# Attention and a SoLU layer on one core: the stationary operands of the two projections get fixed places in SBUF

## The chip, the cores and the metric

The kernel runs on one core of one Trainium2 chip. The metric is the device time of one execution in microseconds (us). Five engines work side by side: TensorE (PE; its weight loads are listed apart as PEld), VectorE (DVE), ScalarE (ACT), GpSimd (POOL) and SyncE (SP, which here only issues transfers). SBUF is the on-chip memory that they read from; a tile has the same byte address in each of its 128 partitions, and "place" below is that address. PSUM is where matmuls write.

## What is computed

The input is q, k, v for a batch of 4, 8 heads, 768 positions and 64 values a head. Each position attends to its neighbours within a window of 16 and to 24 block summaries of the keys (maxima) and values (means). The result is put in rows of 512 values, 3,072 of them, and goes through a layer of two projections:

```python
h = x @ w_in                                   # 3072x512 by 512x1024
e = np.exp(h - h_max)
sm = e / (np.sum(e, axis=-1, keepdims=True) + 1e-09)
solu = h * sm
ln = (solu - mu) / np.sqrt(var + 1e-06) * g_ln
return (ln @ w_out).astype(np.float32)         # 3072x1024 by 1024x512
```

## The kernel before

The 3,072 rows are cut into 24 tiles of 128 rows (t = 0 to 23). For each tile the attention of a quarter of the heads and positions is prepared some tiles ahead: scores (`s`, line 578), a transposition of the exponentials (`t`, line 633), and the values (`x`, line 672). Then `first(t)` (line 686) computes h = x times w_in, the SoLU and the normalization; `turn(t)` (line 750) transposes the normalized rows; and `second(t)` (line 765), four tiles behind, computes the output o.

Both projections work on numbers that are split in an upper part and a lower part, each in a 32-bit format that TensorE takes in one pass. The upper part of x is `xh`, its lower part `xl`; of the normalized rows they are `lh` and `ll`; a weight piece `w` holds both parts, 2,048 bytes each. Three matmuls of 512 columns make one product (lines 697 and 775):

```python
for n, (a, i) in enumerate(((hi, 1), (lo, 0), (hi, 0))):
    nc.tensor.matmul(hp.ap, a.ap[:, c, ts], w.ap[:, i], ...)
```

The first operand (x or the rows) is the stationary one: it is loaded into the array in slices of 128 columns, 512 bytes in a partition. The weight piece is the moving one and streams through. Each tile has 8 such triples in h and 8 in o, so 24 matmuls each.

The order of all work is found ahead of time, in Python. `Plan.op` records each operation with its estimated cost and what it reads and writes; `Plan.order` simulates the engines and orders the operations by due time, in 64 tries with noise; `Plan.issue` (line 141) then emits them in the order of the best try and puts filling matmuls (line 900) where TensorE would idle early on. Costs and due times don't depend on where a tile lies.

`Plan.buf` (line 93) gives each tag a ring of slots. The tile of a slot is made only when it is first used, at `Buf.ap`, and a pool lays its slots one behind the other in that order, each rounded up to 32 bytes. The pool `const` comes first, with a few constants and the 16 weight slots of 4,096 bytes; the pool `sb` lies right behind it. This gives these places, as the remainder of the address by 512:

| tile | slots | remainder by 512 before | used by |
|---|---|---|---|
| w (both parts) | 16 | 96 | h and o, moving |
| xh | 2 | 160, 32 | h; slot by t//2 even, odd |
| xl | 2 | 160, 32 | h; slot by t//2 even, odd |
| lh | 2 | 160, 352 | o; slot by t even, odd |
| ll | 2 | 352, 96 | o; slot by t even, odd |

`lh` and `ll` also take the first value rows that are loaded (`load_v_rows`, line 443), six loads in all, so that the rows of tile t land in slot t mod 2 in both rings. `vacc` (line 496) is a tile of 256 bytes with sums of values.

Of the kernel before, what the change touches and what calls it, by code (L numbers as in the profile page):

```python
# [13 lines left out]
BF16 = mybir.dt.bfloat16  # L14
# [37 lines left out]
class Buf:  # L52


    def __init__(self, make, prev=()):
        self.make, self.prev, self.tile = make, prev, None
        self.ops, self.writers, self.readers, self.gone = [], {}, {}, False
# [15 lines left out]
class Plan:  # L73
# [14 lines left out]
    TRIES, NOISE = 64, 3.0  # L88

    def __init__(self):  # L90
        self.ops, self.rings, self.banks, self.idle = [], {}, {}, None

    def buf(self, pool, shape, dtype, tag, bufs, name):
        ring = self.rings.setdefault(tag, [])
        slot = f"{tag}_{len(ring) % bufs}"
        b = Buf(lambda: pool.tile(shape, dtype, tag=slot, bufs=1, name=name), ring[-bufs:][:1] if len(ring) >= bufs else ())
        ring.append(b)
        return b

    def place(self, make, bank, tag):  # L100

        b = Buf(make, [self.banks[bank]] if bank in self.banks else ())
        self.banks[bank] = b
        self.rings.setdefault(tag, []).append(b)
        return b
# [149 lines left out]
def attn_then_solu(ctx: ExitStack, tc: tile.TileContext, q, k, v, vr, vb, w_in, w_out, g_ln, out):  # L255
# [4 lines left out]
    plan = Plan()  # L260
# [161 lines left out]
    kraw, ksum, vsum, vst, vacc = {}, {}, {}, {}, {}  # L422
    qt, vt, xh, xl, es, ats = {}, {}, {}, {}, {}, {}
# [414 lines left out]
    for t in range(NT):  # L838
        n, j = divmod(t, 2)
        b, g = its[n]  # L840
# [59 lines left out]
        nc.tensor.matmul(x[:, :n], zero[:, :P], zero[:, :n], start=True, stop=True)  # L900

    plan.idle = idle
    plan.issue()


# [38 lines left out]
```

## Time and profile before

| what | us |
|---|---|
| median of 3 runs | 397.99 |
| lowest and highest of the 3 | 396.39 and 946.64 |
| the profiled execution, whole | 397.45 |
| its span in the profile | 395.7 |

The profile is that of one execution. Its span is the time from the first to the last instruction; 1.75 us lie around it. A page gives the busy time of each engine and its share of the span, then the costliest groups of instructions with their count, total and mean in ns, and the idle time in front of them. The chain of waits follows the work back from the last instruction to whatever released it, and lists in order of time where the span went: start, length, engine, tile and line, and how many instructions the piece has. The timeline lists instructions of an engine with start and duration. The busy time by stretches gives for each stretch its length, the busy time of TensorE, its weight loads, VectorE, ScalarE and GpSimd with instruction counts, then the granted TensorE clock, the share of the DMA engines and GB/s.

### The profile page before, as it was taken

How to read it: one execution, taken by the hardware profiler on the slowest of the kernel's cores; microseconds unless marked ns; L12 is line 12 of the kernel's file. 1: busy time of each engine (PE TensorE's matmuls, PEld its weight loads, DVE VectorE, ACT ScalarE, POOL GpSimd, SP SyncE). 2: the span in 40 equal slices, each digit the busy share in tenths (PEclk: the TensorE clock that was granted, in tenths of full speed). 3: DMA queues.
4: the chain of work that ended last, by engine and by line, in shares of the span. 5: the costliest groups of instructions: out<-in, count | busy, mean ns of one | idle time of the engine just before them, and what ended most of it. 6: DMA issues, size and time to landing. Idle time of an engine off the chain costs nothing.

```text
span 395.7 us, 9677 instructions
## 1 busy us (share of the span) xinstructions
PE 386.6 (98%) x3697; PEld 298.3 (75%) x3703; DVE 275.4 (70%) x884; ACT 248.7 (63%) x746; POOL 97.9 (25%) x245
## 2 busy tenths in 40 slices
PE   8999998999999999999999999999999999999996
PEld 3436766677878888878888888878888887878776
DVE  4999998999789866577767657657657654554330
ACT  3889686999798756658558466468466463533411
POOL 4224010416837221236220121221021021101100
PEclk9999999999999999999999999999999999999999
DMA  7999992136277320463330410430310000000011
GB/s 287 411 410 369 409 329 78 56 113 185 70 248 208 113 103 0 141 175 104 123 112 2 150 66 27 156 73 28 108 48 27 2 28 27 16 12 28 27 55 53
DMA packets 14994, 49.24 MB, mean 124 GB/s; under 512 B 1836, under 2 KB 2092, under 8 KB 13412
## 3 DMA queue, kind: packets, MB, share of 16 engines
q1 hardware_dynamic: 11084, 41.89, 30.8%
q10 hardware_dynamic: 3864, 6.74, 4.7%
q8 instruction: 29, 0.48, 0.5%
q14 instruction: 17, 0.14, 0.1%
HBM read 40.11 MB, written 6.29 MB: 117 GB/s over the span
## 4 chain that ended last, share of the span: by engine, by line
PE 85%; DMA 6%; ACT 3%; DVE 2%; issue 1%; ACTq 1%; SPq 1%; DVEq 0%
PE o L775 35%; PE h L697 30%; PE x L672 6%; PE s L578 5%; PE t L633 3%; PE lt L633 3%; DMA st_v<-in_vr 3%; DMA raw<-in_w_in 2%; DMA vt<-vsum 2%; PE vs_ps L459 1%; PE x L900 1%; ACT he L712 1%; DVE he L720 1%; ACT at L281 1%; PE x L664 1%
## 5 line engine op out<-in xcount | busy, mean ns | idle before, releaser
L775 PE MATMUL o<-w,lh 128*128 128x512 f32 (+1 forms) x400 | 128.0, 390 | 0.1
L697 PE MATMUL h<-w,xh 128*128 128x512 f32 x384 | 127.0, 398 | 0.4 <-DVE he L720 0.4
L605 ACT ACTIVATE e<-e,nm 128x120 f32<-128x120 f32 x192 | 73.1, 385 | 25.0 <-DVE nm L597 25.0
L775 PEld LDWEIGHTS o<-w,lh 128*128 128x128 f32 x400 | 74.1, 188 | 18.5 <-issue 2.4
L697 PEld LDWEIGHTS h<-w,xh 128*128 128x128 f32 x384 | 72.1, 188 | 18.9 <-ACT e L605 0.8
L775 PE MATMUL o<-w,ll 128*128 128x512 f32 (+1 forms) x200 | 76.9, 384 | 0.0
L697 PE MATMUL h<-w,xl 128*128 128x512 f32 x192 | 75.6, 394 | 0.0
L707 DVE TENSOR_REDUCE hm<-h 128x1 f32<-128x512 f32 x48 | 32.6, 686 | 42.7 <-PE h L697 42.7
L281 ACT COPY at<-t 120x512 f32<-120x512 f32 x46 | 24.8, 587 | 46.1 <-PE t L633 45.6
L775 PEld LDWEIGHTS o<-w,ll 128*128 128x128 f32 x200 | 37.6, 188 | 6.6
L697 PEld LDWEIGHTS h<-w,xl 128*128 128x128 f32 x192 | 36.1, 188 | 7.5
L597 DVE CUSTOM_DVE_ANT_0 e<-s,mask 128x120 f32<-128x120 f32 x192 | 40.6, 276 | 1.3 <-PE s L578 1.3
L712 ACT ACTIVATE he<-h,hm 128x512 f32<-128x512 f32 x48 | 32.8, 697 | 9.4 <-DVE hm L709 9.4
L605 ACT ACTIVATION_READ_ACCUMULATOR e<-e,nm 128x1 f32 x192 | 36.5, 190 | 0.0
L760 DVE TENSOR_TENSOR ll<-lt,lh 128x512 fp32r<-128x512 f32 x48 | 31.9, 682 | 6.0 <-ACT lh L281 5.8
L739 POOL TENSOR_SCALAR ss<-ss 128x1 f32<-128x1 f32 x24 | 7.1, 297 | 115.0 <-ACT sq L735 114.9
L720 DVE SCALAR_TENSOR_TENSOR he<-h,hz,he 128x512 f32<-128x512 f32 x48 | 34.1, 746 | 0.4
L672 PE MATMUL x<-at,vt 120*64 120x64 f32 (+1 forms) x768 | 28.3, 225 | 1.5 <-ACT at L281 1.5
L672 PEld LDWEIGHTS x<-at,vt 120*64 120x64 f32 (+1 forms) x768 | 24.6, 138 | 6.3 <-ACT at L281 2.8
L288 DVE TENSOR_TENSOR e<-e,z 128x960 f32<-128x960 f32 x23 | 26.6, 1156 | 0.5
L281 ACT CAST lh<-lt 128x512 fp32r<-128x512 f32 x33 | 18.6, 596 | 12.9 <-PE lt L633 10.0
L735 ACT ACTIVATE sq<-he 128x1024 bf16<-128x1024 f32 x24 | 25.2, 1050 | 0.2
(94 smaller groups left out, 499.6 us busy)
## 6 DMA issues: line engine op xcount, KB each, us to landing
vt<-in_v SPq DMA_DIRECT2D x12, 1024.0 KB, 5.4
kraw<-in_k SPq DMA_DIRECT2D x16, 400.0 KB, 9.1
out<-os ACTq DMA_DIRECT2D x23, 256.0 KB, 2.0
qt<-in_q SPq DMA_DIRECT2D x11, 512.0 KB, 5.5
raw<-in_w_in SPq DMA_DIRECT2D x8, 512.0 KB, 10.7
raw<-in_w_out SPq DMA_DIRECT2D x8, 512.0 KB, 9.5
st_v<-in_vr SPq DMA_DIRECT2D x6, 512.0 KB, 12.5
st_v<-in_vb SPq DMA_DIRECT2D x8, 384.0 KB, 3.3
```

Of the source, the lines that this page charges most:

```text
L281: by = {act: lambda: nc.scalar.copy(out=to(), in_=of()), dve: lambda: nc.vector.tensor_copy(out=to(), in_=of()), pool: lambda: nc.gpsimd.t ...
L288: by = {dve: lambda: nc.vector.tensor_tensor(out=to(), in0=a(), in1=b(), op=kind), pool: lambda: nc.gpsimd.tensor_tensor(out=to(), in0=a() ...
L597: nc.vector.tensor_tensor_reduce(out=e.ap[:, n, :], in0=sc.ap[:, j, (2 * i + up) * KC:(2 * i + up + 1) * KC], in1=mask[:, mi, :], scale=-S ...
L605: nc.scalar.activation(out=e.ap[:, n, :], in_=e.ap[:, n, :], func=AF.Exp, bias=nm.ap[:, n:n + 1], scale=-1.0, accum_out=z.ap[:, n:n + 1])
L672: nc.tensor.matmul(xp()[j * D:(j + 1) * D, i, qs], vs.ap[:k, u, cs], at.ap[:k, u % 2, n[j] + u // 2, :], start=not apart, stop=not apart o ...
L697: nc.tensor.matmul(hp.ap, a.ap[:, c, ts], w.ap[:, i], start=(c == 0 and n == 0), stop=(c == NKC - 1 and n == 2))
L707: op(dve, 0.6, lambda i=i, hp=hp: nc.vector.tensor_reduce(out=nms.ap[:, i:i + 1], in_=hp.ap, op=ALU.max, axis=AX.X, negate=True), r=[hp], ...
L712: op(act, 0.71, lambda i=i, hp=hp: nc.scalar.activation(out=part(i), in_=hp.ap, func=AF.Exp, bias=nm.ap, accum_out=zs.ap[:, i:i + 1]), r=[ ...
L720: op(dve, 0.67, lambda i=i, hp=hp: nc.vector.scalar_tensor_tensor(out=part(i), in0=hp.ap, scalar=zs.ap[:, 0:1], in1=part(i), op0=ALU.mult, ...
L735: op(act, 1.13, lambda: nc.scalar.activation(out=sq.ap, in_=e.ap, func=AF.Square, accum_out=ss.ap), r=[e], w=[sq, ss])
L760: op(dve, 0.6, lambda part=part, r=r: nc.vector.tensor_tensor(out=part(lo), in0=tp.ap[:, r], in1=part(hi).bitcast(F32), op=ALU.subtract), ...
L775: nc.tensor.matmul(o.ap[:, cols], a.ap[:, f, :], w.ap[:, i, cols], start=(f == 0 and n == 0), stop=(f == NFC - 1 and n == 2))
```

## The change

Before anything is emitted, the first tile of each slot is now made in a fixed order: the 16 weight slots, then `ll` and `xl` with two slots each, one slot of `vacc` with its 256 bytes, then `lh` and `xh`, and then all others in the order in which the plan asked for them. The slots of the pool `sb` start at a remainder of 96. So `ll` and `xl` lie at 96, and behind the 256 bytes of `vacc` the slots of `lh` and `xh` lie at 352, all by 512. The weight slots keep the remainder 96. Nearly all other tiles get other addresses too: for instance the queries go from 416 and 160 to 160 and 416, the exponentials stay at 96, and the tiles `he` go from a mix of 160, 96 and 384 to 416. The two PSUM tiles with tag `s` are made ahead of the single banks. No operation is added, removed or given another cost.

```diff
     def __init__(self):
-        self.ops, self.rings, self.banks, self.idle = [], {}, {}, None
+        self.ops, self.rings, self.banks, self.idle, self.slots = [], {}, {}, None, []
 
     def buf(self, pool, shape, dtype, tag, bufs, name):
         ring = self.rings.setdefault(tag, [])
         slot = f"{tag}_{len(ring) % bufs}"
         b = Buf(lambda: pool.tile(shape, dtype, tag=slot, bufs=1, name=name), ring[-bufs:][:1] if len(ring) >= bufs else ())
+        if len(ring) < bufs:
+            self.slots.append((tag, math.prod(shape[1:]) * (2 if dtype == BF16 else 4), b))
         ring.append(b)
         return b
+
+    def lay_out(self):
+        slots = list(self.slots)
+        for tag, n in (("w", 16), ("ll", 2), ("xl", 2), ("vacc", 1), ("lh", 2), ("xh", 2), ("", 99)):
+            mine = [x for x in slots if x[0] == tag or not tag or (tag == "w" and x[0][1:].isdigit())][:n]
+            for x in mine:
+                slots.remove(x)
+                x[2].ap
...
     plan.idle = idle
+    plan.lay_out()
     plan.issue()
```

## The prediction

> **What bounds the kernel now.** I read the page first, then the busy time by stretches of the span, then the chain of waits in order of time, and last the timeline of TensorE inside single tiles. The page and the stretches:
>
> ```profile
> span 395.7 us, 9677 instructions
> PE 386.6 (98%) x3697; PEld 298.3 (75%) x3703; DVE 275.4 (70%) x884; ACT 248.7 (63%) x746; POOL 97.9 (25%) x245
> ...
> PE 85%; DMA 6%; ACT 3%; DVE 2%; issue 1%; ACTq 1%; SPq 1%; DVEq 0%
> ...
> L775 PE MATMUL o<-w,lh 128*128 128x512 f32 (+1 forms) x400 | 128.0, 390 | 0.1
> L697 PE MATMUL h<-w,xh 128*128 128x512 f32 x384 | 127.0, 398 | 0.4 <-DVE he L720 0.4
> ...
> 80.00:125.00 45.00, 44.30 (x507) 34.43 (x503) 39.63 (x123) 39.78 (x118) 23.43 (x48) 1.00 0.56 173
> 125.00:380.00 255.00, 254.99 (x2341) 207.11 (x2340) 161.92 (x527) 144.04 (x440) 53.97 (x146) 1.00 0.21 68
> ```
>
> From 125 to 380 us TensorE is busy for 254.99 of 255.00 us at a granted clock of 1.00, and no other engine is above 64% (VectorE, 161.92 of 255). So there each ns that a matmul gives up is a ns of the kernel, as long as the others keep up. Before 125 us it also waits for loads and for the other engines. What fills the bound stretch are the two projections: h (line 697) and o (line 775), 24 matmuls of 512 columns for each of the 24 row tiles. They are 400+384 plus half as many with the lower parts, 1,176 instructions.
>
> A matmul's duration (390, 398 ns) overlaps its neighbours, so what counts is the distance between starts. A triple of matmuls (upper x lower weights, lower x upper, upper x upper) is one period. The timeline of TensorE, first and last of five rows at the same place of five triples, in four tiles; columns are start and duration in us:
>
> ```profile
> 253.87 0.61 PE L775 MATMUL o<-w,lh 128*128 128x512 f32 x2
> ...
> 256.59 0.61 PE L775 MATMUL o<-w,lh 128*128 128x512 f32 x2
> ...
> 269.51 0.62 PE L775 MATMUL o<-w,lh 128*128 128x512 f32 x2
> ...
> 272.28 0.62 PE L775 MATMUL o<-w,lh 128*128 128x512 f32 x2
> ...
> 260.54 0.63 PE L697 MATMUL h<-w,xh 128*128 128x512 f32 x2
> ...
> 263.33 0.63 PE L697 MATMUL h<-w,xh 128*128 128x512 f32 x2
> ...
> 303.97 0.62 PE L697 MATMUL h<-w,xh 128*128 128x512 f32 x2
> ...
> 306.71 0.62 PE L697 MATMUL h<-w,xh 128*128 128x512 f32 x2
> ```
>
> Four triples take 2.72 us in o of tile 11, 2.77 in o of tile 12, 2.79 in h of tile 16, 2.74 in h of tile 19. That is 0.680, 0.693, 0.698 and 0.685 us a triple, for instructions that are the same but for the buffers they read (a tile's number is found by counting off 24 matmuls a tile from the first h and the first o). The buffers alternate: o by t, h by t//2. So the place of a buffer is worth up to 0.018 us a triple, 2.6%. The whole tiles in the chain of waits (start, us) show the same split:
>
> ```profile
> 127.04 5.59 PE h L697 x24
> ...
> 133.75 1.08 PE x L672 x32
> ...
> 135.81 5.66 PE o L775 x24
> ...
> 149.27 0.98 PE s L578 x32
> 150.25 5.75 PE o L775 x24
> ...
> 164.78 5.71 PE o L775 x24
> ...
> 171.49 5.70 PE h L697 x24
> ...
> 186.22 5.49 PE h L697 x24
> ...
> 238.19 5.79 PE o L775 x24
> ...
> 259.34 5.79 PE h L697 x24
> ...
> 297.16 4.39 PE o L775 x18
> 301.56 0.70 PE h L697 x3
> 302.26 1.40 PE o L775 x6
> 303.66 4.83 PE h L697 x21
> ...
> 325.15 5.75 PE o L775 x24
> 330.90 5.60 PE h L697 x24
> ...
> 338.23 5.66 PE o L775 x24
> ...
> 350.02 5.79 PE o L775 x24
> 355.82 5.51 PE h L697 x24
> ```
>
> **Which places are which.** By the program's allocation each of the 16 weight slots lies at 96 behind a multiple of 512 bytes, and so do both its halves (2,048 bytes apart). The stationary slices are 512 bytes wide, so all slices of a buffer share its remainder. Before: (upper, lower) = (160, 352) for o of even t, (352, 96) for o of odd t, (160, 160) for h of t//2 even, (32, 32) for h of t//2 odd. The rows of tile 11 and of 135.81 and 338.23 (tiles 3 and 17) are odd t: the pair (352, 96) is the fastest of the four, 0.680 a triple, and the beat is the same for all eight of its 512-byte slices, so the remainder decides and not a higher address bit. The change gives exactly this pair to every tile of both projections. So its price needs no guess about why some places are slow: it stands in the trace.
>
> **The change part by part.** It removes and adds no instruction. The planner's costs and dues know no address, so the order on each engine, the queues of SP and ACT and the waits stay; I count 0 for them.
>
> o: a tile after the small matmuls becomes 5.66. Even tiles from 125 us on: four at 5.75 (the first and last are 150.25 and 325.15), -0.09 each, -0.36; two at 5.79 (238.19, 350.02), -0.26; tile 14 in two pieces, 4.39+1.40 = 5.79, -0.13; tiles 6, 20 and 22 lie in pieces that the chain mixes with neighbours, and I take -0.13 for each, as 14, -0.39. Together -1.14. Odd tiles: 0.
>
> h: a tile that directly follows o keeps the beat and should take 8 x 0.680 = 5.44. Eight such tiles are at 5.59 or 5.60 (first 127.04, last 330.90), -0.16 each, -1.28; seven are of the pair (160, 160), and 127.04, tile 7, is the one tile of (32, 32) among them. Six are at 5.49 to 5.51 (first 186.22, last 355.82), -0.05 to -0.07 each, -0.34. Tile 19, 0.70+4.83 = 5.53, gives -0.09. Two follow other work, so they start anew and should match o's 5.66: 259.34 at 5.79, -0.13, and 171.49 at 5.70, -0.04. Together -1.88.
>
> Before 125 us: nine tiles of the slower pairs at up to the same 0.16 or 0.09 could give about 0.8 if TensorE bound there. Its ends are 0 and -0.8. Between 80 and 125 us it is busy 44.30 of 45.00 us, and four of these tiles lie there, so I take half, -0.4.
>
> The other tiles that move: the small matmuls also read buffers in two places (queries, windows of keys, exponentials), and the chain's rows for x (1.08) and s (0.98) are the same for all of them; 0. Operands of VectorE, ScalarE and GpSimd and the landing places of loads move too. What place is worth to them no row shows by itself; the nearest is VectorE's subtraction into `ll` (ns: least, median, most), which already works on both slots of `lh` and `ll`:
>
> ```profile
> L760 DVE TENSOR_TENSOR ll<-lt,lh x48: 640/682/692, 72.6 to 383.9; 128x512 fp32r<-128x512 f32 x48
> ```
>
> It bounds the effect at 10 ns of 682 slower or 42 faster, 1.5% and 6%. On VectorE's 161.92 us of the stretch that is 2.4 us more or 10 less, beside 93 us in which it has nothing to do; I take 0, and without that cover it would be those 2.4. What comes late next when TensorE gains 3 us of 255 is the softmax of h (ScalarE and VectorE), and with 36% of the stretch free it is not near.
>
> Sum: -1.14 - 1.88 - 0.4 = -3.4 against the profiled execution's 397.45 us (span 395.7): 394.0 us. That execution lies 0.54 below the median of the three runs, 397.99.
>
> **A rule against the change.** The Trainium skill, page "TensorE: Matmul & The Clock Gate", section "Step-by-step: what each phase is for", says that TensorE has two independent SBUF read ports and that "Loading the next tile's weights doesn't steal SBUF read bandwidth from the running matmul". By that rule placement would be worth nothing and the time would stay at 397.45. The rows above (0.680 against 0.698 a triple) do not agree with it: something in the placement is paid for, so I give that outcome little.
>
> **The rivals.**
> Nothing changes: the load of the next slice and the stream of the running matmul never meet, and the split by parity comes from something else that alternates. Against it: h alternates in pairs of tiles and o singly, just as their buffers do. 397.45 us; chance 0.11. This is the outcome that the section of the Trainium skill named above would lead to.
>
> Slower: the beat is not fixed by the pair alone. The pair (160, 352) shows 5.75 in four tiles and 5.79 in others, and tile 7 has 5.59 where its pair has 5.49 elsewhere. So one pair can settle in two rhythms, and which one it finds is decided in the first few starts of a tile. If (352, 96) falls into the worst of them from its new neighbours, o takes 5.79 and h behind o 5.60: odd o tiles 10 x +0.13, the four at 5.75 +0.16, the six fast h tiles +0.11 each, tile 19 +0.07 and 171.49 +0.09. That is +2.3, so 399.7 us. Against it: the eight odd o tiles that stand whole in the chain read 5.66 to 5.71 (164.78, the slowest, found the rhythm late), so none stayed in a slow one. Chance 0.08.
>
> Much faster: 0.680 a triple, 0.227 a matmul, is still not the least the array shows. The filling matmuls of 512 columns in bf16:
>
> ```profile
> 78.24 1.46 PE L900 MATMUL x<-zero 128*128 128x512 bf16 x6
> ...
> L900 PE MATMUL x<-zero 128*128 128x512 bf16 x21 | 5.4, 381 | 0.2 <-issue 0.2
> ```
>
> (1.46 - 0.38)/5 = 0.216 us. If having all tiles at the pair frees the rest of the conflict, some 38 tiles from 125 us on gain another 24 x 0.011 = 0.26 each, 9.9 us: 384.1 us. Against it: the odd o tiles already read only operands at the new places, and they run at 0.227. Chance 0.06.
>
> **How the numbers follow.** The forecast has 0.75. Its own range is 393.6 (all 0.8 of the early part) to 396.3 (h gives nothing, so that only o's 1.14 comes). The range in which I want 8 in 10 also takes in most of the unchanged case and the spread of the two close runs shown (396.39 and 397.99, so about 0.8 to either side): 392.2 to 398.0. A 2% change, 389.5 or 405.4, is about what a measurement of this kernel can tell from no change. Only the much faster rival passes it downward, 0.06. Upward none does by the rows; I keep 0.03 of the slower rival for a rhythm worse than any row shows. Same: 0.91.
>
> **What would show it.** In the chain of the changed kernel all o tiles read 5.66 and all h tiles behind o 5.44; the rows at 5.75 and 5.79 are gone. Steps of the timeline are 0.68 a triple in both projections, and the mean of a matmul of 128x512 falls below 398 and 400 ns. The rows for x and s stay at 1.08 and 0.98. Odd o tiles, which read nothing that has a new remainder, must not move; if they do, the remainder isn't what counts. If h stays at 5.60 while o falls, the place of the moving operand or a direct handover matters. If TensorE is no longer busy throughout 125 to 377 us, another engine took over the gain.

## The result

The changed kernel takes 393.75 us (median of 4 runs, 393.44 to 394.00); the kernel before takes 397.39 us (median of 4). The ratio is 0.992, with a 95% interval of 0.990 to 0.994; it leaves out the one run of 946.64 us of the kernel before. The profiled execution took 394.00 us, 3.45 less than the one before, and its span fell from 395.7 to 392.3 us.

Page and stretches of the changed kernel, with the same columns as before. Line 709 is what was 697, line 787 what was 775:

```profile
span 392.3 us, 9677 instructions
...
PE 383.3 (98%) x3697; PEld 298.2 (76%) x3703; DVE 276.4 (70%) x884; ACT 248.6 (63%) x746; POOL 97.4 (25%) x245
...
L787 PE MATMUL o<-w,lh 128*128 128x512 f32 (+1 forms) x400 | 127.3, 389 | 0.1
L709 PE MATMUL h<-w,xh 128*128 128x512 f32 x384 | 125.5, 394 | 0.4 <-DVE he L732 0.4
```

```profile
125.00:378.00 253.00, 252.86 (x2344) 207.47 (x2343) 161.08 (x526) 143.47 (x438) 54.17 (x146) 1.00 0.21 69
```

Instruction counts are the same. TensorE is still busy almost throughout (252.86 of 253.00 us) and VectorE, ScalarE and GpSimd do the same work in the same time within 0.6%. So no other engine took the gain.

In the timeline of TensorE, first and last of five triples, o of tile 11 and h of tile 15:

```profile
252.07 0.62 PE L787 MATMUL o<-w,lh 128*128 128x512 f32 x2
...
254.80 0.62 PE L787 MATMUL o<-w,lh 128*128 128x512 f32 x2
```

```profile
243.23 0.62 PE L709 MATMUL h<-w,xh 128*128 128x512 f32 x2
...
245.95 0.62 PE L709 MATMUL h<-w,xh 128*128 128x512 f32 x2
```

Four triples now take 2.73 us in o and 2.72 in h, 0.68 each; before, o took 2.72 or 2.77 and h 2.74 or 2.79. The chain of waits shows whole tiles (start, length in us, engine, tile, line, instructions):

```profile
126.39 5.46 PE h L709 x24
131.84 0.13 issue
131.97 0.69 PE t L645 x16
...
133.16 1.08 PE x L684 x32
...
135.23 5.71 PE o L787 x24
140.93 5.44 PE h L709 x24
...
149.55 5.66 PE o L787 x24
155.21 5.44 PE h L709 x24
...
193.71 5.71 PE o L787 x24
...
236.59 5.66 PE o L787 x24
242.26 5.44 PE h L709 x24
...
257.55 5.66 PE h L709 x24
...
352.79 5.44 PE h L709 x24
```

All h tiles behind an o tile from 125 us on are at 5.44 or 5.46, where 5.49 to 5.60 stood. The o tiles that stand whole are at 5.66 or 5.67, but for 135.23 and 193.71 with 5.71; 5.75 and 5.79 are gone.

### The profile page after: what moved, and what is told of

Its sections match the earlier page's. It is cut to its first block, busy times and chain, and to the rows that moved or that the text cites. A ratio compares the mean times of both kernels' runs of the same rounds, so it can differ in the third digit from the quotient of the medians.

```text
span 392.3 us, 9677 instructions
## 1 busy us (share of the span) xinstructions
PE 383.3 (98%) x3697; PEld 298.2 (76%) x3703; DVE 276.4 (70%) x884; ACT 248.6 (63%) x746; POOL 97.4 (25%) x245
## 4 chain that ended last, share of the span: by engine, by line
PE 85%; DMA 6%; DVE 4%; ACT 3%; issue 1%; ACTq 1%; SPq 1%; DVEq 0%
PE o L787 35%; PE h L709 29%; PE x L684 6%; PE s L590 5%; PE t L645 3%; PE lt L645 3%; DMA st_v<-in_vr 3%; DMA raw<-in_w_in 2%; PE vs_ps L471 1%; DMA vt<-vsum 1%; PE x L912 1%; DVE he L732 1%; ACT at L293 1%; PE x L676 1%; ACTq L497 1%
## 5 line engine op out<-in xcount | busy, mean ns | idle before, releaser
L709 PE MATMUL h<-w,xh 128*128 128x512 f32 x384 | 125.5, 394 | 0.4 <-DVE he L732 0.4
L709 PE MATMUL h<-w,xl 128*128 128x512 f32 x192 | 74.8, 390 | 0.0
L751 POOL TENSOR_SCALAR ss<-ss 128x1 f32<-128x1 f32 x24 | 7.9, 330 | 112.8 <-ACT sq L747 112.7
L300 DVE TENSOR_TENSOR e<-e,z 128x960 f32<-128x960 f32 x23 | 27.6, 1202 | 0.5
L740 POOL TENSOR_SCALAR he<-he,nmu 128x512 f32<-128x512 f32 x11 | 11.3, 1024 | 57.1 <-DVE nmu L735 57.1
```

The source lines that it names most:

```text
L300: by = {dve: lambda: nc.vector.tensor_tensor(out=to(), in0=a(), in1=b(), op=kind), pool: lambda: nc.gpsimd.tensor_tensor(out=to(), in0=a() ...
L709: nc.tensor.matmul(hp.ap, a.ap[:, c, ts], w.ap[:, i], start=(c == 0 and n == 0), stop=(c == NKC - 1 and n == 2))
```

## The experiments

All kernels start from the changed one. "Distance" is the remainder of a stationary buffer less that of the weights, by 512. The change has distance 256 for the upper part and 0 for the lower, written (256, 0). The layouts were made with a list of places and small unused gap tiles in front of a slot:

```diff
+    PLACES = (("ll", 1, 96), ("lh", 0, 160), ("xh", 0, 160), ("xl", 0, 160), ("lh", 1, 352), ("ll", 0, 352), ("xh", 1, 32), ("xl", 1, 32))
-    def lay_out(self):
+    def lay_out(self, pool, at=96):
...
+        for tag, i, place in self.PLACES:
+            if place != at:
+                pool.tile([P, (place - at) % 512 // 4], F32, tag=f"gap_{tag}_{i}", bufs=1, name=f"gap_{tag}_{i}")
```

**Is it these buffers, or the rest that moved?** The list above gives the eight stationary buffers their old remainders, while all other tiles, and the PSUM tiles, keep the new order. The gaps move those other tiles too: by 512, the exponentials lie at 288 and `he` at 96, where the change has 96 and 416.

> All tiles are laid out in the new fixed order, but the stationary buffers get back the remainders they had before: (upper, lower) = (160, 352) and (352, 96) for the rows, (160, 160) and (32, 32) for x; everything else is moved as in the change. Theory (the pair of remainders alone decides): the time is that of before, 397.4 us within 1, with o tiles alternating between 5.66 and 5.75 to 5.79 us and h behind o between 5.49 and 5.60. Rival (the move of the other tiles or of the PSUM tiles made the gain): about 393.8 us, all o tiles 5.66 and all h tiles 5.44.

396.96 us against 397.24 for the kernel before (ratio 0.9996, 0.998 to 1.001). Its chain of waits:

```profile
208.08 5.80 PE o L795 x24
213.88 5.60 PE h L717 x24
...
222.65 5.67 PE o L795 x24
228.31 5.49 PE h L717 x24
...
236.98 5.75 PE o L795 x24
```

The old values are back, by kind of tile. Single tiles changed between the two values of their kind: o of tile 8 takes 5.80 here and 5.75 before, o of tile 10 takes 5.75 and 5.79, h of tile 11 takes 5.59 and 5.49. So each of these two slow pairs has two beats. Such a move of everything else is worth nothing that can be measured (the interval leaves room for some 0.8 us), so the gain lies in the eight buffers.

**One projection at a time.** First only the rows get the new pair, then only x.

```diff
+    PLACES = (("ll", 0, 96), ("ll", 1, 96), ("xh", 0, 160), ("xl", 0, 160), ("lh", 0, 352), ("lh", 1, 352), ("xh", 1, 32), ("xl", 1, 32))
```

> Only the rows get the new pair (352, 96); x keeps (160, 160) and (32, 32). Theory (each projection pays for its own pair): o tiles 5.66, h tiles behind o still 5.49 and 5.60, so some 1.3 us of the 3.6 are gained: 396.1 us. Rival (the rhythm is handed over from o to h and o sets it): h falls too, towards 5.44, and the time is near 394.

```diff
+    PLACES = (("ll", 1, 96), ("xl", 0, 96), ("xl", 1, 96), ("lh", 0, 160), ("lh", 1, 352), ("ll", 0, 352), ("xh", 0, 352), ("xh", 1, 352))
```

> Only x gets the new pair (352, 96); the rows keep (160, 352) for even and (352, 96) for odd tiles. Theory: h behind o 5.44 to 5.5, o alternates between 5.66 and 5.75 to 5.79; some 2.3 us are gained: 395.1 us. Rival (handover): h behind an even o tile keeps a slow beat of 5.60 and only h behind odd o tiles gets 5.44, so near 396.5.

The rows alone: 395.76 us, ratio 0.9957 (0.994 to 0.997). x alone: 395.09 us, ratio 0.9939 (0.992 to 0.996). Chain of waits, rows alone:

```profile
200.36 5.60 PE h L717 x24
...
209.14 5.67 PE o L795 x24
```

and x alone:

```profile
209.33 5.75 PE o L795 x24
215.08 5.44 PE h L717 x24
...
223.70 5.67 PE o L795 x24
229.37 5.44 PE h L717 x24
```

With the rows alone h stays at 5.60 although the o in front of it is fast; with x alone h is at 5.44 even behind a slow o of 5.75. So no rhythm is handed over: each projection pays for its own buffers. The two gains, 1.5 and 2.2 us, add up to the whole within their intervals. By 512, the rows alone differ from the kernel with the old pairs in the places of the rows' buffers and of the few value loads that share them, and of nothing else: 395.76 against 396.96 us. With x alone the other tiles lie, by 512, where the change has them, but for those loads and `vacc`.

**Distance or absolute place.** The weights and all eight buffers are moved by 224 bytes.

```diff
+    const.tile([P, 56], F32, name="gap_w")
+    PLACES = (("ll", 0, 320), ("ll", 1, 320), ("xl", 0, 320), ("xl", 1, 320), ("lh", 0, 64), ("lh", 1, 64), ("xh", 0, 64), ("xh", 1, 64))
```

> Weights, rows and x are all moved by the same 224 bytes: weights at remainder 320, upper parts at 64, lower parts at 320, so that the distances between them are those of the change. Theory (the distance between the slice that is loaded and the weights that stream counts): same as the change, 393.8 us within 0.8, o 5.66, h behind o 5.44. Rival (the absolute remainder counts): beats of 0.685 to 0.70 us a triple appear, 395 to 400 us.

394.02 us, ratio 0.991 (0.989 to 0.994), and in the chain:

```profile
207.08 5.67 PE o L796 x24
212.75 5.44 PE h L718 x24
```

None of the eight buffers and no weight slot lies where it lay in the change, by 512, and the tiles read the same: whole o tiles 5.66 to 5.71, h behind o 5.44. What counts is the distance, as far as one such shift can show.

**Which distances are good.** Three kernels hold four pairs each, one for each kind of tile, seen once.

```diff
+    PLACES = (("lh", 0, 96), ("ll", 0, 96), ("xh", 0, 96), ("xh", 1, 224), ("xl", 1, 224), ("lh", 1, 352), ("ll", 1, 352), ("xl", 0, 352))
```

> Four pairs in one kernel, given as distance (upper, lower) from the weights' remainder, where the change has (256, 0): o even (0, 0), o odd (256, 256), h of t//2 even (0, 256), h of t//2 odd (128, 128). Theory A (each load pays by its own distance, and 0 and 256 are free): the first three settle at 0.680 us a triple, the fourth at 0.69 or more. Rival B (upper and lower must lie half of 512 apart, wherever they are): (0, 256) settles at 0.680, while (0, 0), (256, 256) and (128, 128) take 0.685 to 0.70, as (64, 64) and (448, 448) did before.

```diff
+    PLACES = (("xl", 0, 128), ("lh", 0, 288), ("ll", 0, 288), ("xh", 1, 320), ("xh", 0, 384), ("lh", 1, 416), ("ll", 1, 416), ("xl", 1, 64))
```

> Four more pairs, as distance (upper, lower) from the weights: o even (192, 192), o odd (320, 320), h of t//2 even (288, 32), h of t//2 odd (224, 480). Theory A (0 and 256 are free, other distances are paid for): all four at 0.685 to 0.70 us a triple. Rival B (half of 512 apart is what counts): the two pairs of h settle at 0.680 and the two of o do not.

```diff
+    PLACES = (("lh", 0, 192), ("ll", 0, 192), ("lh", 1, 256), ("ll", 1, 256), ("xh", 0, 448), ("xl", 0, 448), ("xh", 1, 0), ("xl", 1, 0))
```

> Four more pairs, as distance (upper, lower) from the weights: o even (96, 96), o odd (160, 160), h of t//2 even (352, 352), h of t//2 odd (416, 416). Theory (so far 64 and 320 both gave 0.700 us a triple, 192 and 448 both 0.687, 0 and 256 both 0.680: only the distance by 256 counts): o even and h of t//2 even settle alike, since 352 = 96+256, and o odd and h of t//2 odd settle alike, since 416 = 160+256. Rival (the period is 512): they differ by 0.005 us a triple or more. None is expected below 0.680.

The times were 395.51, 398.73 and 400.39 us, beside 398.03, 398.03 and 397.00 for the kernel before. From the first kernel's chain, o of tiles 7 and 8 and h of tiles 13 and 14:

```profile
194.15 5.71 PE o L795 x24
...
208.47 5.66 PE o L795 x24
214.14 5.44 PE h L717 x24
...
228.43 5.59 PE h L717 x24
```

From the second's, o of tiles 7 and 8 and h of tiles 13 and 14:

```profile
195.14 5.79 PE o L795 x24
...
209.70 5.72 PE o L795 x24
215.43 5.60 PE h L717 x24
...
230.00 5.60 PE h L717 x24
```

From the third's timeline, first and last of five triples in o and in h of even kind:

```profile
210.91 0.63 PE L795 MATMUL o<-w,lh 128*128 128x512 f32 x2
...
213.73 0.63 PE L795 MATMUL o<-w,lh 128*128 128x512 f32 x2
...
216.54 0.63 PE L717 MATMUL h<-w,xh 128*128 128x512 f32 x2
...
219.35 0.64 PE L717 MATMUL h<-w,xh 128*128 128x512 f32 x2
```

Four triples take 2.82 and 2.81 us. In one table, with the whole tiles of the chains from 125 us on; an o tile is some 0.2 us longer than h at the same pair, because it starts anew:

| distance (upper, lower) | o, us | h behind o, us |
|---|---|---|
| (0, 0) | 5.66 to 5.69 | |
| (256, 256) | 5.67 to 5.71 | |
| (256, 0) the change | 5.66 to 5.71 | 5.44 to 5.47 |
| (0, 256) | | 5.44 |
| (192, 192) and (448, 448) | 5.70 to 5.72 | 5.49 to 5.51, twice 5.59 |
| (64, 256) even rows before, with the old pairs and with x alone | 5.75 to 5.80 | |
| (64, 64) and (320, 320) | 5.79 to 5.80 | 5.60 |
| (128, 128) | | 5.57 to 5.59 |
| (288, 32); (224, 480) | | 5.60; 5.59 to 5.60 |
| (160, 160) and (416, 416) | 5.80 | 5.60 to 5.61 |
| (96, 96) and (352, 352) | 5.81 to 5.82 | 5.62 to 5.63 |

So upper and lower need not lie apart: (0, 0) and (256, 256) are as good as the change, and (288, 32), just as far apart as the change's pair, is not. Distances that differ by 256 give the same: it is the distance by 256 that counts, and of the multiples of 32 only 0 is free. That each load pays for its own distance is only in part shown: in the one mixed pair, (64, 256), the lower load lies at a good place, and part of the tiles take 5.75, others 5.79 or 5.80 as with both loads at 64.

**Finer steps.** The slots are made 32 bytes wider and the view inside is shifted by 4, 8 or 16 bytes.

```diff
+    SHIFT = {'lh_0': 4, 'll_0': 4, 'lh_1': 2, 'll_1': 2, 'xh_0': 4, 'xl_0': 4, 'xh_1': 1, 'xl_1': 1}
...
+                x = pool.tile([P, 1032], dtype, tag=slot, bufs=1, name=name)[:, k:k + 1024]
+                return x.rearrange("p (a b) -> p a b", a=shape[1])
```

> Four pairs close to the good places, as distance (upper, lower) from the weights: o even (16, 16), o odd (8, 8), h of t//2 even (240, 240), h of t//2 odd (4, 4). Theory (places are told apart in units of at least 32 bytes, as far as the scans went): 4, 8 and 16 stay at 0.680 us a triple, 240 (just below 256) pays 0.685 or more. Rival (0.680 is itself a slow beat between finer steps): one of them falls below 0.680, towards 0.648.

397.61 us, the kernel before 398.88. Chain of waits (o of tiles 7, 8; h of tiles 13, 14; o of tile 18):

```profile
194.95 5.74 PE o L800 x24
...
209.35 5.80 PE o L800 x24
215.15 5.49 PE h L722 x24
...
229.56 5.58 PE h L722 x24
...
350.33 5.65 PE o L800 x24
```

The expectation was wrong. Distance 16 takes 5.80, 8 takes 5.74, 4 takes 5.58 and 240 takes 5.49: a single 4-byte element off the multiple of 256 already brings h to 5.58, more than three quarters of all that a wrong place costs in h (5.44 to 5.60 or 5.62). No h tile lies below 5.44. One o tile stands out: tile 18, at distance 16 like tile 8, takes 5.65 at 350.33, as good as the best place; its triples are 0.68 us apart in the timeline. It is the one whole tile seen that found the best beat at a bad distance, and no run shows why. Whether a start off a 32-byte boundary costs something by itself isn't told apart here, as the weights stayed on theirs.

**Is it the load's reads?** With the layout of the second scan each load in o takes the first column of its slice 128 times over.

```diff
-                            o.ap[:, cols], a.ap[:, f, :], w.ap[:, i, cols], start=(f == 0 and n == 0),
+                            o.ap[:, cols], a.ap[:, f, 0:1].broadcast_to([P, P]), w.ap[:, i, cols], start=(f == 0 and n == 0),
```

> The places of the second scan (distance (192, 192) for o even, (320, 320) for o odd), but in o each load takes the first column of its slice 128 times, at the same place, instead of 128 columns, so that the load reads 4 bytes over and over; the output is then not that of the reference. Theory (the slice that is loaded and the weights that stream meet as both walk through memory): the beat of o no longer depends on the pair, both kinds of tiles settle alike, at 0.680 us a triple or less. If it falls to about 0.648 (the filling matmuls' 0.216 each), the load's reads are the whole rest too; if it stays at 0.680, the rest belongs to the matmul itself. Rival (the start address alone counts): 0.687 and 0.700 us stay.

398.44 us, the kernel before 398.88. In the chain, o of tiles 7 and 8, which were 5.79 and 5.72 with whole slices:

```profile
195.05 5.75 PE o L795 x24
...
209.57 5.75 PE o L795 x24
```

Half of the expectation held: the two pairs no longer differ, so at these two distances it is where the load's 128 reads go that makes the difference, not its start alone. The other half failed: the beat doesn't fall to the best one, it lies between the two.

**Is the rest of 0.227 us the load's too?** With the layout of the change, the first matmul of each triple in o (but a tile's first) loads 64 columns only.

```diff
+                        m = QT if f and not n else P
-                            o.ap[:, cols], a.ap[:, f, :], w.ap[:, i, cols], start=(f == 0 and n == 0),
+                            o.ap[:m, cols], a.ap[:, f, :m], w.ap[:, i, cols], start=(f == 0 and n == 0),
```

> The layout of the change, but in o the first matmul of each triple but the first one of a tile loads only 64 of the 128 columns and writes 64 rows; the product of the upper part with the lower weights is left out for the other 64 rows. Theory (the rest of 0.227 over the filling matmuls' 0.216 is also paid for the load's reads): the triple of o falls from 0.680 to about 0.669 and h stays at 0.680. Rival (0.227 belongs to the stream of the 512 columns): o stays at 0.680 or above.

395.30 us in one run. Chain of waits:

```profile
214.31 5.44 PE h L709 x24
...
222.93 5.72 PE o L788 x24
228.65 5.45 PE h L709 x24
```

7 of the 24 loads of a tile are halved and o gets slower, 5.72 for 5.66; h, untouched, stays. So the theory falls: shorter loads don't bring the beat below 0.227. The halved matmuls also write 64 rows for 128, and whether that or the uneven loads slow the beat isn't told apart.

**All at a bad place.** The eight buffers at distance 64.

```diff
+    PLACES = (("lh", 0, 160), ("lh", 1, 160), ("ll", 0, 160), ("ll", 1, 160), ("xh", 0, 160), ("xh", 1, 160), ("xl", 0, 160), ("xl", 1, 160))
```

> All eight stationary buffers at distance 64 from the weights, the slowest distance seen. Theory: every tile settles at 0.700 us a triple, o 5.79 and h behind o 5.60; from the tiles of before that is +2.3 us in the stretch in which TensorE is the bound and up to +0.5 ahead of it: 399.5 to 400 us against 397.2. Rival (other engines or the start of a tile absorb it): 397 to 398.5.

399.91 us against 397.00, ratio 1.007 (1.005 to 1.009):

```profile
210.67 5.79 PE o L795 x24
216.47 5.60 PE h L717 x24
```

The tiles' prices give the right time in the other direction as well (399.5 to 400 was expected). Between the best and this place lie about 6 us, 1.5% of the kernel, for the same instructions in the same order.

## Why the prediction was right

The sum, -3.4 us on the profiled execution's 397.45, gave 394.0; the profiled execution took 394.00 and the median is 393.75. Step by step:

- That a tile's beat is set by the places of its stationary buffers, and that the move of all else costs 0: shown by the old remainders in the new layout (0.9996) and by the chain's rows for x, still 1.08.
- The o term, even tiles to 5.66: those that stand whole read 5.66. The h term, 5.44 behind o and 5.66 after other work: 5.44 to 5.46, and 257.55 with 5.66. That the pair's price could be read off the odd o tiles was right, since x alone and the rows alone show it for each.
- Before 125 us I took -0.4 between 0 and -0.8. Tile 7's h starts at 126.39 instead of 127.04, -0.65. The chain's first o row starts at 74.85 instead of 75.20, so 0.35 of that came before it and 0.30 after it. The chain ahead of it runs through loads, ScalarE and VectorE, and the start of the bound stretch moves between executions whatever the layout: tile 7's h starts at 125.82 with the old pairs and at 127.67 with x alone. So two profiles don't settle this term.
- In the stretch the sum was -2.9 (without tile 22, which ends later). From tile 7's h to the o piece near the end (374.74 before, 371.48 after) the starts moved by 3.26, so 2.61 came there. The 0.3 that is missing stands in rows: 135.23 and 193.71 take 5.71 and not 5.66 (0.10), and tile 7's h is followed by 0.13 of issue and a transposition of 0.69 instead of 0.62. The statement that odd o tiles must not move was too strict by these two: their triples too settle at 0.68 in the timeline, only some starts later than in other tiles. That the 0.25 too much ahead of tile 7 and the 0.3 too little behind it offset each other, so that the profiled execution hits 394.00, is luck.
- That "the remainder decides" was right as far as the trace went and coarser than the truth: it is the distance to the weights, by 256, and down to 4 bytes. Nor does it decide alone: two slow pairs have two beats each, which tiles swap between kernels at the same places, and one tile at distance 16 ran at the best beat.

The rival "nothing changes" fell with the pair of runs at the old places and at distance 64. It is what the Trainium skill, "TensorE: Matmul & The Clock Gate", section "Step-by-step: what each phase is for", implies, where loading the next weights takes nothing from the running matmul; the measured 5.44 to 5.62 us for the same 24 matmuls by the place of the loaded slices do not agree with that for these 32-bit operands. No run shows that it is read bandwidth that is lost. The slower rival's price, 399.7, is nearly that of distance 64 (399.91), but its condition, that the good pair settles in a slow rhythm from new neighbours, didn't occur. Its premise, that one pair can settle in two rhythms, holds for two of the slow pairs. The much faster rival fell too: no distance tried, nor a shorter load, brought the beat below 0.227.

What stays open is the unit in which load and stream meet. The runs show that the distance counts by 256, that 0 is best, and that reading one element over and over costs the same at the two distances tried; they don't show which part of the memory or of TensorE makes one wait for the other, nor why some slow pairs have two beats, nor what the 11 ns over the filling matmuls are.

## What to carry to other kernels

Where TensorE is the bound and streams 512 columns of 32-bit operands behind loads of 128 columns, compare the distance of starts between tiles that alternate buffers: if it alternates with them, place may be what is paid for, and moving the buffers alone tells. Put the stationary slices at a multiple of 256 bytes from the moving operand; the price of not doing so was up to 3% of the distance between starts here, and 1.5% of the kernel. A trace that holds the new condition somewhere already, as the odd tiles did, prices a change without a theory of why.

## What was not expected of the hardware

One element, 4 bytes, off the multiple of 256 costs most of what the worst place costs (5.58 against 5.44 and 5.62 us for 24 matmuls). Halving 7 of a tile's 24 loads made the tile slower (5.72 against 5.66). Loads that read a single column make the two places tried alike at 5.75, slower than a good place with whole slices. And a slow place isn't slow in the same way each time: the even rows at (64, 256) take 5.75 in some tiles and 5.80 in others, and one tile at distance 16 took 5.65.
